# A fused block with 32 heads on one core: values projected as columns and turned by transposes, partly inside the attention, and the front in a new order

## The chip, the cores and the metric

The kernel runs on one core of one Trainium2 chip. Its engines work side by side, each through its own queue of instructions in order: TensorE (PE, with its weight loads shown as PEld), VectorE (DVE), ScalarE (ACT), GpSimd (POOL), and SyncE (SP), whose queue issues all DMAs here. The metric is the device time of one execution in microseconds (us), as the median of several. Lower is better.

## What is computed

The input x has 2048 tokens of 512 columns. A condition c gives six vectors of 512. They shift and scale two layer norms and weigh two residual branches: attention with 32 heads of 16 columns, then a dense layer with GELU and 1792 inner columns.

```python
mod = (_silu(c) @ w_mod).reshape(c.shape[0], 6, 1, -1)
sa, ca, ga, sb, cb, gb = (mod[:, i] for i in range(6))
h = _layernorm(x) * (1 + ca) + sa
qkv = h @ wqkv                      # q, k, v: 32 heads of 16
p = softmax(q k^T * 16 ** -0.5)     # per head, over all 2048 keys
x = x + ga * ((p v) @ wo)
h = _layernorm(x) * (1 + cb) + sb
x = x + gb * (gelu(h @ w1 + b1) @ w2 + b2)
```

All of it is float32. Matmul operands are split into a high and a low part, and three of the four products are added (`terms3`), so a projection of 512 contraction rows is 4 x 3 = 12 matmuls of 128 rows: a group. A group adds up in one PSUM bank of 128 partitions by 512 columns.

## The kernel before

**Front (lines 438 to 547).** For each of four blocks of 512 tokens: `ln1` takes the statistics of the x rows (VectorE, one power on GpSimd) and scales them, `ln1_t` turns them with 16 transposes and evicts them as the high and low parts of h^T (`hT`). Then `proj_qk` forms 128 columns of keys or queries (a chunk, 8 heads) for 512 tokens, with the columns in the partitions, splits them and stores them to DRAM (`qk_d`). `proj_v` forms values for 128 tokens and all 512 columns, with the tokens in the partitions, so four groups serve a block; ScalarE copies each into `vst` (two tiles in turn), which also holds a column of ones per head, and every second copy is stored to `v_d`. All 512 columns of the value weights are loaded at the start into the second x tile (line 185), split by `split_v` and kept in `wv`. The second block of x is loaded into the same tile later (`load_x(1)`, line 485), behind the key and query transfers of the first block.

`quad` (453) runs four groups at once on half the rows: two groups work on opposite halves, and between every 8 half matmuls it may run `mx_pair`: two score matmuls (line 393) whose row maximum VectorE reduces (398). The banks come from rings: `pr` (0, 1, 2, 6, 7) for the front, `mx` (3, 4, 5) for those scores. `XFIRST` orders the first 64 score matmuls of each half. The front ends with 88 of them done (`LEAD`). The maxima of a unit go through DRAM into two extra rows of the query tile, which meet rows of ones (`one_rows`) in the key tiles, so that the exponent is already shifted.

**Attention (lines 551 to 983).** 32 units (four query blocks x eight groups of four heads) of 16 steps, 128 keys each. A step has four score matmuls with an exponential each (589, 594), four score matmuls for the maxima of later units, four products with the values (`pv`, 618), and up to six half matmuls of background work (`RUN`). The background runs through `work()`: `block0` (the remaining keys and queries, 22 groups), then the FFN of blocks 0 to 2. `later(n, f)` runs f after n ticks; a tick is an exponential, so four make a step. `step_start` issues the loads of coming units: first keys at step 1 of a unit, queries at 2, values at 3, second keys at 9. At every third step `prep` loads a piece of wo, w1 or w2, scales and splits it and stores it to DRAM. `open_ffn` (631) frees the memory of the projections for the FFN once `block0` and all `prep` are through. `o_prep` divides an attention output by its sum of exponentials through DRAM (`dn`, `rden`, `rb`); `try_prep` starts one when none is at work (`busy`).

**Tail (from line 986).** What is left of the FFN of block 2 is run together with the last block.

Of the kernel before, what the change touches and what calls it, by code (L numbers as in the profile page):

```python
# [38 lines left out]
XFIRST = [x for r in range(4) for x in [(0, r * 8 + i) for i in range(8)] + [(1, r * 3 + i) for i in range(3)]]  # L39
XFIRST += [(1, i) for i in range(12, 32)]  # L40
RUN = 6
WB = 8
PARTS = ((0, 6), (6, 12), (12, NF))
# [6 lines left out]
def block_kernel(ctx: ExitStack, tc: tile.TileContext, x, wqkv, wo, w1, b1, w2, b2, c, w_mod, out):  # L50
# [78 lines left out]
    wq = [wpool.tile([P, 2, 2, KC, P], FR, name=f"wqk{i}") for i in range(2)]  # L129
    scm, spool = pool("stage", side="right")  # L130
    vcm, vpool = pool("vproj", side="right")
    wv = vpool.tile([P, 2, KC, D], FR, name="wv")
    vst = [vpool.tile([P, NG, 2, VG], F32, name=f"vst{i}") for i in range(2)]

    def stage(name):
        return spool.tile([P, D], F32, tag="s2", name=name, bufs=4)
# [16 lines left out]
    raws = {}  # L153

    def load_w(k):
        raw = pieces("wraw", F32).rearrange("p w (k n) -> p w k n", n=P)
        for w in (1, 0):
            sy.dma_start(raw[:, w], wq_r[:, :, w * D + k * P : w * D + (k + 1) * P])
        raws[k] = raw

    def split_w(k, fast=False):
        raw = raws.pop(k)
        t = wq[k % 2]
        for w in (1, 0):
            if fast:
                ve.tensor_copy(t[:, 0, w], raw[:, w])
                ve.tensor_tensor(t[:, 1, w], raw[:, w], t[:, 0, w].bitcast(F32), op=ALU.subtract)
            else:
                ac.activation(t[:, 0, w], raw[:, w], AF.Copy)
                gp.tensor_tensor(t[:, 1, w], raw[:, w], t[:, 0, w].bitcast(F32), op=ALU.subtract)  # L170

    def split_v():
        for i in range(KC):
            r = xin[1][:, i]
            ac.activation(wv[:, 0, i], r, AF.Copy)
            eng = gp if i % 2 else ve
            eng.tensor_tensor(wv[:, 1, i], r, wv[:, 0, i].bitcast(F32), op=ALU.subtract)
# [5 lines left out]
    load_w(0)  # L183
    for i in range(KC):
        sy.dma_start(xin[1][:, i], wq_r[:, i, 2 * D :])
# [10 lines left out]
    for t in vst:  # L196
        gp.memset(t[:, :, :, 4 * VW :], 0.0)
        for j in range(4):
            gp.memset(t[:, :, :, j * VW + DH], 1.0)
# [5 lines left out]
    def mod_copy(ps):  # L205
        r = stage("mrow")
        ac.activation(r, ps, AF.Copy)
        return r
# [43 lines left out]
    def ln1_t(b, rows, between=lambda: None):  # L252
# [10 lines left out]
        def evac():  # L263
            for fc in range(KC):
                h = stage("h32")
                ac.activation(h, pss[fc], AF.Identity, scale=modc[:, 0, fc, 0:1], bias=modc[:, 0, fc, 1:2])
                e1, e2 = (ve, (ve, gp)[fc % 2]) if b == 0 else (gp, gp)
                e1.tensor_copy(hi[:, fc], h)
                e2.tensor_tensor(lo[:, fc], h, hi[:, fc].bitcast(F32), op=ALU.subtract)
# [7 lines left out]
    def later(n, f):  # L277
        hooks.setdefault(clock["t"] + n, []).append(f)

# [29 lines left out]

    def proj_qk(bk, w, k, b, fast=False):  # L310
        hi, lo = hT[b]
        t = wq[k % 2]

        def evac(ps):
# [4 lines left out]
            else:  # L319
                r = stage("pf")  # L320
                ac.activation(r, ps, AF.Copy)  # L321
                gp.tensor_copy(parts[:, 0], r)  # L322
                gp.tensor_tensor(parts[:, 1], r, parts[:, 0].bitcast(F32), op=ALU.subtract)
            if bk == "bg":
                later(8, lambda: store_qk(w, k, b, parts))
            else:
                store_qk(w, k, b, parts)

        n = range(KC)
        return terms3([t[:, 0, w, i] for i in n], [t[:, 1, w, i] for i in n],  # L330
                      [hi[:, i] for i in n], [lo[:, i] for i in n]), bk, evac

    def proj_v(bk, b, t):
        hi, lo = hT[b]
        sl = slice(t * P, (t + 1) * P)
        kc = b * 4 + t
        v = vst[(kc // 2) % 2]

        def evac(ps):
            ac.activation(v[:, :, t % 2, : 4 * VW].rearrange("p g (j e) -> p g j e", e=VW)[:, :, :, :DH],  # L340
                          ps.rearrange("p (g j d) -> p g j d", j=4, d=DH), AF.Copy)
            if t % 2:
                sy.dma_start(v_d[:, :, kc - 1 : kc + 1, :].rearrange("g p k e -> p g k e"), v)

        n = range(KC)
        return [(hi[:, i, sl], wv[:, j, i]) for i in n for j in range(2)] + [(lo[:, i, sl], wv[:, 0, i]) for i in n], bk, evac
# [85 lines left out]
    def mx_pair():  # L432
        seen = [f() for f in [mx_mm(1), mx_mm(0)]][0]
# [7 lines left out]
    split_w(0, fast=True)  # L441
# [9 lines left out]
    split_v()  # L451
    sy.dma_start(one_d.rearrange("a (x y) -> a x y", y=128), ones[:, None, :].to_broadcast([2, HS // 128, 128]))
    def quad(groups, visits):
# [20 lines left out]

    for b in range(NB):
        run(proj_qk("pr", 1, 0, b, fast=True))
        if b == 0:
            run(proj_qk("pr", 0, 0, 0, fast=True))
        for u in range(2):
            if u == 0 or b < 2:  # L480
                load_k(u, b // 2, (b % 2) * TB, (b % 2 + 1) * TB)
            if b == 0:
                load_q(u)
        if b == 0:
            load_x(1)
        if b + 2 < NB:
            load_x(b + 2)
# [556 lines left out]
```

## Time and profile before

| | |
|---|---|
| median of 3 runs | 1810.22 us (1810.06 to 1820.29) |
| profiled execution | 1813.47 us, span 1811.7 us |
| TensorE busy | 1745.2 us |
| VectorE busy | 1395.3 us |
| ScalarE busy | 1210.0 us |
| first score matmul of the attention proper | at 157.85 us |
| first and last unit's output copied | at 209.72 and 1673.89 us |

The profile lists instructions by engine and source line. A timeline row holds the start, the time, engine, line, operation, the tile written and the tiles read, the shapes, the number of merged instructions, and in brackets how long the engine had been idle and what released it. A row of a group (from the list by lines) holds the total and the mean duration behind the bar. PEclk is the clock that TensorE was granted, as a share of the full one. SP's rows are DMA issues, not transfers. In PE rows the ends are modelled, so starts are compared.

### The profile page before, as it was taken

What the parts mean: (1) busy time and instruction counts of PE and PEld (TensorE: products, weight loads), DVE (VectorE), ACT (ScalarE), POOL (GpSimd) and SP (SyncE); (2) the same over time, 40 slices, a digit from 0 to 9 for tenths busy, and PEclk for the clock granted to TensorE, in tenths of its full rate; (3) what the DMA queues carried; (4) which work ended last, traced back from release to release, by engine and by line L of the source; (5) the groups of instructions that cost most, each with busy time, mean ns of one, the idle gap of its engine ahead of it and who ended that gap; (6) DMA issues with size and microseconds to landing.
All of it is one profiled execution on the core that took longest, in us unless ns stands there. A gap on an engine that the chain in (4) does not pass through costs nothing. (4 is left out here: it accounts for less than half of the span.)

```text
span 1811.7 us, 32267 instructions
## 1 busy us (share of the span) xinstructions
PE 1745.2 (96%) x12020; PEld 902.8 (50%) x12020; DVE 1395.3 (77%) x2341; ACT 1210.0 (67%) x2303; POOL 613.8 (34%) x646
## 2 busy tenths in 40 slices
PE   7698999999999999999999999999999999999899
PEld 5474444444334444444444444444444444444677
DVE  4466888888899888888889988888889988850232
ACT  2424777777677678778776678777777678777031
POOL 2413545443100256306420156405510046503620
PEclk8798999999899999999999999999999999999899
DMA  6648777777653434445447444436546434312544
GB/s 196 202 123 197 206 199 194 205 194 188 174 112 78 84 86 104 84 102 145 114 98 203 100 97 107 91 73 155 120 95 179 117 84 107 91 42 85 201 163 162
DMA packets 122906, 242.62 MB, mean 134 GB/s; under 512 B 30982, under 2 KB 50454, under 8 KB 122750
## 3 DMA queue, kind: packets, MB, share of 16 engines
q1 hardware_dynamic: 122750, 240.57, 51.9%
q8 instruction: 95, 1.56, 0.4%
q14 instruction: 61, 0.50, 0.1%
HBM read 187.61 MB, written 52.90 MB: 133 GB/s over the span
## 5 line engine op out<-in xcount | busy, mean ns | idle before, releaser
L398 DVE TENSOR_REDUCE mxp<-mx 128x1 f32<-128x512 f32 x2048 | 1272.5, 682 | 197.6 <-PE mx L393 168.4
L594 ACT ACTIVATE p<-e 128x512 f32<-128x512 f32 x1964 | 1025.7, 603 | 365.6 <-PE e L589 313.4
L393 PE MATMUL mx<-kh,qst 48*128 48x512 f32 x2048 | 872.0, 443 | 18.6 <-DVE mxp L398 12.3
L589 PE MATMUL e<-qst,kh 50*128 50x512 f32 x1964 | 716.9, 420 | 7.2 <-issue 6.8
L618 PE MATMUL pv<-p,vg 128*32 128x512 f32 x4096 | 549.3, 608 | 0.0
L589 PEld LDWEIGHTS e<-qst,kh 50*128 50x128 f32 x1964 | 357.4, 187 | 178.8 <-ACT p L594 156.1
L393 PEld LDWEIGHTS mx<-kh,qst 48*128 48x128 f32 x2048 | 374.4, 186 | 71.5 <-DVE mxp L398 63.1
L287 PE MATMUL bg<-w,g 64*128 64x512 f32 (+1 forms) x1008 | 271.2, 406 | 2.9 <-DVE x L841 0.4
L287 PE MATMUL bg<-pc,w 64*128 64x512 f32 (+1 forms) x972 | 266.2, 407 | 1.0 <-ACT p L594 0.7
L287 PEld LDWEIGHTS bg<-w,g 64*128 64x128 f32 (+1 forms) x1008 | 177.1, 186 | 144.4 <-ACT p L594 82.2
L287 PEld LDWEIGHTS bg<-pc,w 64*128 64x128 f32 (+1 forms) x972 | 167.6, 184 | 156.9 <-ACT p L594 96.4
L618 PEld LDWEIGHTS pv<-p,vg 128*32 128x32 f32 x4096 | 81.0, 108 | 128.7 <-issue 120.5
L412 POOL CAST m<-mt 128x32 fp32r<-128x32 f32 x32 | 6.7, 210 | 383.3 <-DVE mt L410 383.3
L287 PE MATMUL bg<-hThi,wqk 64*128 64x512 f32 x352 | 107.4, 424 | 0.3 <-ACT p L594 0.3
L815 POOL TENSOR_SCALAR s<-s 128x512 f32<-128x512 f32 x42 | 62.8, 1496 | 128.7 <-ACT s L813 117.9
L287 PEld LDWEIGHTS bg<-hThi,wqk 64*128 64x128 f32 x352 | 59.6, 188 | 80.6 <-ACT p L594 72.2
L287 PE MATMUL bg<-wo,pc 64*128 64x512 f32 x288 | 82.0, 412 | 1.0
L808 POOL TENSOR_TENSOR s<-h 128x512 f32<-128x512 f32 x42 | 43.7, 1040 | 94.1 <-ACT h L807 94.0
L287 PEld LDWEIGHTS bg<-wo,pc 64*128 64x128 f32 x288 | 49.5, 184 | 47.5 <-ACT p L594 27.7
L670 POOL TENSOR_TENSOR ob<-ob,rb 128x512 f32<-128x512 f32 x12 | 15.4, 1284 | 166.8 <-DMA rb<-rden 152.0
L322 POOL CAST parts<-pf 128x512 fp32r<-128x512 f32 x27 | 16.5, 610 | 116.6 <-ACT pf L321 106.3
L816 POOL TENSOR_TENSOR h<-s,h 128x512 f32<-128x512 f32 x42 | 54.0, 1286 | 3.5
(127 smaller groups left out, 1268.5 us busy)
## 6 DMA issues: line engine op xcount, KB each, us to landing
kh<-qk SPq DMA_DIRECT2D x366, 128.0 KB
w<-w1s SPq DMA_DIRECT2D x56, 512.0 KB
w<-w2s SPq DMA_DIRECT2D x50, 512.0 KB
vg<-v SPq DMA_DIRECT2D x32, 664.0 KB
qk<-parts SPq DMA_DIRECT2D x32, 512.0 KB
qst<-qk SPq DMA_DIRECT2D x192, 64.0 KB
ou<-osb SPq DMA_DIRECT2D x32, 256.0 KB
wo<-wos SPq DMA_DIRECT2D x16, 512.0 KB
```

Source lines behind the costliest of these rows:

```text
L287: return te.matmul(ps, term[0][r], term[1][r], start=i == 0, stop=i == n - 1)
L322: gp.tensor_copy(parts[:, 0], r)
L393: te.matmul(ps, qst[u][r0 : r0 + KR, p, qc * P : (qc + 1) * P], kh(u, kr // 2)[r0 : r0 + KR, p, (kr % 2) * TB : (kr % 2 + 1) * TB], start= ...
L398: ins = ve.tensor_reduce(mxp[u][:, hc, kr : kr + 1], ps, axis=AX.X, op=ALU.max, negate=True)
L412: gp.tensor_copy(m2[:, 0], mt)
L589: te.matmul(ps, kh(u, kc // 8)[r0 : r0 + KX, p, (kc % 8) * P : (kc % 8 + 1) * P], qst[u][r0 : r0 + KX, p], start=True, stop=True)
L594: saw(ac.activation(t, ps, AF.Exp, scale=SCALE))
L618: te.matmul(cur["ps"][32 * j : 32 * (j + 1)], vg[u][:, kc, j * VW : j * VW + 32], pt.pop(4 * s + j), start=kc == 0, stop=kc == NKC - 1)
L670: eng.tensor_tensor(ob, ob, rb, op=ALU.mult)
L808: gp.tensor_tensor(s, h, h, op=ALU.mult)
L815: gp.tensor_scalar(s, s, 1.0, None, op0=ALU.add)
L816: gp.tensor_tensor(h, s, h, op=ALU.mult)
```

## The change

Values are now projected like keys and queries: a chunk of 128 columns (8 heads) for 512 tokens, columns in the partitions, the weight chunk stationary. ScalarE copies the bank to an SBUF row tile (`vr`), and `turn_v` turns that by four transposes into one bank, from which two ScalarE copies fill the only tile `vst`, and one DMA stores it. Of the 16 value groups, 8 (chunks 0 and 1) run in the front, 8 (chunks 2 and 3) in the background of the attention; there a turn takes a bank of the `mx` ring and its store goes out 4 ticks later. The queries of blocks 1 and 2 for chunk 0 move from the background to the front. `block0` now follows a plan of 28 groups over ten weight chunks, each loaded two chunks ahead and split 12 ticks later into one of four slots.

The front is no longer a loop over blocks: block 0 with one value group, then `ln1` of blocks 1 and 2, then four quads with keys, values and queries mixed, a last value group and its turns; the last keys, the ones and the values of unit 0 are loaded behind them. The second block of x is loaded at the start. For blocks 1 to 3 the high part of h^T is made by ScalarE from PSUM; front groups' high parts of keys and queries too (both before by GpSimd). `stage` has a tag per use instead of four shared tiles, the tiles of exponentials go from 12 to 10, unit loads are issued at steps 1, 5, 8 and 12, `prep` works 8 ticks after its load, two `o_prep` may be at work, and a callable job of the background no longer uses up its half step.

```diff
-    wq = [wpool.tile([P, 2, 2, KC, P], FR, name=f"wqk{i}") for i in range(2)]
+    wslots = [wpool.tile([P, 2, KC, P], FR, name=f"wqkv{i}") for i in range(4)]
+    vst = wpool.tile([P, 2, 4, VG], F32, name="vst")
...
-    wv = vpool.tile([P, 2, KC, D], FR, name="wv")
-    vst = [vpool.tile([P, NG, 2, VG], F32, name=f"vst{i}") for i in range(2)]
+    wfirst = vpool.tile([P, 2, KC, P], FR, name="wqkv4")
...
-    load_w(0)
-    for i in range(KC):
-        sy.dma_start(xin[1][:, i], wq_r[:, i, 2 * D :])
+    for w in (1, 0):
+        load_w(w, 0)
+    load_x(1)
...
-                e1, e2 = (ve, (ve, gp)[fc % 2]) if b == 0 else (gp, gp)
-                e1.tensor_copy(hi[:, fc], h)
-                e2.tensor_tensor(lo[:, fc], h, hi[:, fc].bitcast(F32), op=ALU.subtract)
+                if b:
+                    ac.activation(hi[:, fc], pss[fc], AF.Identity, scale=modc[:, 0, fc, 0:1], bias=modc[:, 0, fc, 1:2])
+                else:
+                    ve.tensor_copy(hi[:, fc], h)
+                (gp if b or fc % 2 else ve).tensor_tensor(lo[:, fc], h, hi[:, fc].bitcast(F32), op=ALU.subtract)
...
+    def proj_v(bk, k, b):
+        def evac(ps):
+            r = stage("vr")
+            ac.activation(r, ps, AF.Copy)
+            vrows.append((k, b, r, clock["t"]))
+        return proj_terms(2, k, b), bk, evac
+
+    def turn_v(bk):
+        k, b, r, _ = vrows.pop(0)
+        ps = take(bk)
+        for t in range(4):
+            te.transpose(ps[:, t * P : (t + 1) * P], r[:, t * P : (t + 1) * P], ident)
+        v = vst
+        p5 = ps.rearrange("p (t g j d) -> p g t j d", t=4, g=2, d=DH)
+        for g in range(2):
+            ac.activation(v[:, g, :, : 4 * VW].rearrange("p t (j e) -> p t j e", e=VW)[:, :, :, :DH], p5[:, g], AF.Copy)
+        def store():
+            vstored.add((k, b))
+            sy.dma_start(v_d[2 * k : 2 * k + 2, :, 4 * b : 4 * b + 4, :].rearrange("g p k e -> p g k e"), v)
+        if bk == "mx":
+            soon(4, store)
+        else:
+            store()
...
-    for b in range(NB):
...
+    run(proj_qk("pr", 1, 0, 0, fast=True))
+    run(proj_qk("pr", 0, 0, 0, fast=True))
...
+    run(vals(0, 0))
+    rows = ln1(1)
+    ln1_t(1, rows)()
+    load_x(3)
+    rows = ln1(2)
+    turn_v("pr")
+    split_w(1, 1, wslots[1])
+    load_w(2, 1)
+    for _ in range(3):
+        mx_pair()
+    ln1_t(2, rows)()
...
+    quad([keys(1, 0, 1), vals(0, 1), keys(1, 1, 0), keys(1, 1, 1)], [mx_pair] * 3 + [third] + [mx_pair] * 7 + [None])
...
+    ln1_t(3, rows)()
+    turn_v("pr")
...
+    quad([keys(1, 0, 2), vals(0, 2), keys(1, 0, 3), vals(0, 3)], [mx_pair] * 9 + [ahead, mx_pair, None])
...
+    turn_v("pr")
+    turn_v("pr")
+    quad([keys(1, 1, 2), keys(1, 1, 3), keys(0, 1, 0), vals(1, 0)], [mx_pair] * 11 + [None])
...
+    turn_v("pr")
+    quad([vals(1, 1), vals(1, 2), keys(0, 0, 1), keys(0, 0, 2)], [mx_pair] * 8 + [None] * 4)
+    turn_v("pr")
+    turn_v("pr")
+    run(vals(1, 3))
+    turn_v("pr")
...
-    ppcm, ppool = pool("p", bufs=12)
+    ppcm, ppool = pool("p", bufs=10)
...
-        assert not preps and not any(hooks)
+        assert not preps and not owed[0]
...
-        if (unit >= NU - 2 + k // 2 if b == NB - 1 else free_pc[0] >= b) and not busy[0]:
+        if (unit >= NU - 2 + k // 2 if b == NB - 1 else free_pc[0] >= b) and busy[0] < 2:
...
+        plan = [(1, 2, range(NB)), (0, 2, [0]), (2, 2, range(NB)), (1, 3, range(NB)), (0, 3, [0]), (2, 3, range(NB))]
+        plan += [(0, 0, [3])] + [(0, k, range(1, NB)) for k in range(1, KC)]
...
+                while vrows and clock["t"] >= vrows[0][3] + 4:
+                    yield lambda: turn_v("mx")
...
-        if kc == 2 and u + 2 < NU:
+        if kc == 5 and u + 2 < NU:
             load_q(u + 2)
-        if kc == 3 and u + 1 < NU:
+        if kc == 8 and u + 1 < NU:
             load_v(u + 1)
-        if kc == 9 and u + 2 < NU:
+        if kc == 12 and u + 2 < NU:
             load_k(u + 2, 1)
```

`soon` is `later` with a count of what is still owed, on which `open_ffn` now waits instead of on every hook; `keys(w, k, b)` and `vals(k, b)` are `proj_qk` and `proj_v` in the front's ring; `third` is a `mx_pair` with `ln1(3)` behind it, `ahead` one with a key load before it.

245 lines of the change are left out of this document (115 added, 130 removed).

## The prediction

> **What bounds the kernel now.** I read the page's busy times first, then a table of stages (windows), then the timeline around each hole that the table shows, and last the waits of the DMA queue.
>
> ```profile
> span 1811.7 us, 32267 instructions
> PE 1745.2 (96%) x12020; PEld 902.8 (50%) x12020; DVE 1395.3 (77%) x2341; ACT 1210.0 (67%) x2303; POOL 613.8 (34%) x646
> ```
>
> The stages:
>
> ```profile
> 38.00:49.00 11.00, 0.33 (x1) 0.18 (x1) 5.02 (x14) 1.20 (x2) 1.01 (x1) 0.59 0.90 283
> 49.00:71.00 22.00, 16.46 (x70) 10.45 (x69) 3.00 (x10) 13.00 (x19) 13.48 (x15) 0.66 0.61 184
> 71.00:92.00 21.00, 15.98 (x120) 12.74 (x119) 17.18 (x35) 4.15 (x7) 5.74 (x6) 0.92 0.63 203
> 150.30:157.90 7.60, 0.75 (x6) 0.35 (x5) 0.69 (x1) 0.70 (x2) 1.78 (x3) 0.66 0.74 274
> 209.70:256.40 46.70, 46.70 (x354) 22.79 (x356) 40.08 (x67) 35.66 (x70) 21.20 (x23) 1.00 0.77 199
> 441.70:491.00 49.30, 46.38 (x258) 18.86 (x260) 40.47 (x69) 33.84 (x66) 5.48 (x7) 0.90 0.71 181
> 491.00:535.00 44.00, 42.15 (x258) 16.67 (x260) 40.27 (x68) 33.52 (x66) 4.93 (x7) 1.00 0.48 103
> ```
>
> The first score and the first product with values (pv):
>
> ```profile
> 157.85 0.76 PE L589 MATMUL e<-qst,kh 50*128 50x512 f32 x1 [6.85 <-issue]
> 164.29 0.20 PEld L618 LDWEIGHTS pv<-p,vg 128*32 128x32 f32 x8 [0.65 <-issue]
> ```
>
> Columns of a window: length, then busy time of PE, PEld, DVE, ACT and POOL, granted clock, DMA share, GB/s. TensorE bounds most of it. A unit of the attention (16 steps) with background work in every step takes 46.70 us, all of it PE (2.92 a step); the unit without any takes 44.00 (2.75 a step). The front, up to the first score at 157.85, has three holes: 38 to 49, the half clock after it, and 150 to 158.
>
> **The front, followed through.** Its rows:
>
> ```profile
> 25.77 2.02 PE L287 MATMUL pr<-wv,hThi 128*128 128x512 f32 x8
> 42.16 0.69 DVE L227 BATCH_NORM_STATS2 bst<-xin 128x6 f32<-128x512 f32 x1 [14.86 <-DMA xin<-in_A_x_dram]
> 47.80 2.93 ACT L249 ACTIVATE xin<-xin,nb,rs 128x512 f32<-128x512 f32 x4 [10.03 <-DVE nb L247]
> 48.67 0.18 PEld L260 LDWEIGHTS pr<-ident,xin 128*128 128x128 f32 x1 [11.98 <-ACT xin L249]
> L266 ACT ACTIVATE h<-pr,modc 128x512 f32<-128x512 f32 x16 | 11.9, 776 | 2.6 <-DVE modc L216 1.4 <-PE pr L260 0.6
> L269 POOL TENSOR_TENSOR hTlo<-h,hThi 128x512 fp32r<-128x512 f32 x14 | 18.4, 1315 | 10.6 <-DVE hThi L268 9.6
> L232 POOL TENSOR_TENSOR rs<-rs,mhalf 128x4 f32<-128x4 f32 x4 | 4.1, 1014 | 30.5 <-DVE rs L231 30.5
> 84.42 0.28 PEld L393 LDWEIGHTS mx<-kh,qst 48*128 48x128 f32 x1 [5.46 <-DVE mxp L398]
> 91.96 2.11 PE L287 MATMUL pr<-hThi,wqk 128*128 128x512 f32 x8
> 94.82 1.91 PE L260 MATMUL pr<-ident,xin 128*128 128x128 f32 x16
> 113.95 1.92 PE L203 MATMUL pr<-wm,s_m 128*32 128x512 f32 x16
> 118.59 1.20 PE L287 MATMUL pr<-wv,hThi 64*128 64x512 f32 x8
> 132.60 0.39 PE L287 MATMUL pr<-hThi,wqk 64*128 64x512 f32 x1
> ```
>
> Prices from them: a group of 12 full matmuls 2.86 us (91.96 to 94.82); a quad of four groups with 22 score matmuls 14.0 (118.59 to 132.60), 1.17 a visit; 16 transposes 1.9; a modulation with its broadcast 4.6 (113.95 to 118.59).
>
> Keys and queries of block 0 stay, to 25.7. Four value groups become one: PE is done at 28.6. The second block of x now takes the place of the value weights in the first loads, so VectorE starts its statistics behind the query's subtraction at about 27.3, not at 42.16; 5.2 us later (47.80 less 42.16, less a DMA wait of 0.45) the rows are scaled, and the transposes start at 33.4. The hole of 11.5 us shrinks to 4.9. Then other engines set the pace. Each part of h passes ScalarE twice (0.78 each, the high part no longer on POOL) and POOL once (1.3); block 2's power waits on POOL behind four such subtractions: 42.4 (36.2 and eight passes) + 1.3, then the power 1.0 and the factors 0.5, give 45.3. Its transposes end near 50.2; the first quad starts at 51.3 when a ring bank is free. It keeps the stall that the row at 84.42 shows, since statistics still sit among the score reductions (some 4.3 of 5.5; x is there earlier), with an estimated 3.5 for the clock at its start and after the stall (its window of 21.0 us holds 14.0 of work and 5.5 of stall, so 1.5 went there, and now it starts cold): 51.3 + 14.0 + 7.8 = 73. The second quad waits for bank evictions: two key groups (four passes of 0.6), one split (0.65) and four of block 3's passes on ScalarE: start 79, end 93.5. Modulation and two turns 4.7, third quad 14: 112. Modulation with broadcast and a turn 5.1: 117.5. The last quad has 8 visits with scores and 4 without: 13.2, to 130.7.
>
> Behind it comes a chain that is new. The values are turned through one tile (before: two), so a turn's copies wait until the previous store has read it.
>
> ```profile
> 96.37 0.36 SPq L308 DMA_DIRECT2D qk<-parts  x1
> 99.35 2.66 SPq L364 DMA_DIRECT2D kh<-qk  x6
> 136.29 5.38 SPq L364 DMA_DIRECT2D kh<-qk  x6
> 141.71 6.62 SPq L370 DMA_DIRECT2D kh<-one  x10
> 154.95 0.57 SPq L423 DMA_DIRECT2D qst<-m  x2
> L340 ACT ACTIVATE vst<-pr 128x512 f32<-128x512 f32 x16 | 9.0, 600 | 36.7 <-PE pr L287 22.7 <-issue 14.0
> ```
>
> A store lands some 2.5 us after its issue (96.73 to 99.35). Three turns are left: copies 0.8 (two halves of the 0.60 row's size, estimated at 0.4 each), issue 0.4, landing 2.5, so 3.7 each. First store at 135.2 (behind the query evictions), third at 142.6. Behind it the same queue issues the last keys (5.4 us) and the ones (6.6), then the value load. The first pair of ones lands near 151.6 (issue to use 2.3 us, from 155.52 to 157.85): first score 6 us earlier than 157.85. The value load goes out at 155 and is larger; at 4 us it lands at 159.3, and the first pv matmul, wanted at 158.0, runs there instead of at 164.29. **Front: -5.0 us.** The maxima of unit 0 are done by 126 now, so their transfer, on which 157.85 waited, is hidden.
>
> **Background in the attention.** Eight value groups come in, two query groups (blocks 1 and 2 of chunk 0) go to the front: 6 x 24 = 144 half matmuls, and one group less is left for the tail (24): 168, at 6 a step 28 steps, from 2.75 to 2.92 us. **+4.6 us.** They fill the steps between the end of the projections and the FFN of block 0, which waits for unit 7 either way; it starts no later.
>
> **Turns in the attention.** Eight, each 4 transposes: 1.91/4 = 0.48 us on a PE that has no room. Their ScalarE copies (0.8) fit a gap:
>
> ```profile
> 175.74 0.60 ACT L594 ACTIVATE p<-e 128x512 f32<-128x512 f32 x1 [0.85 <-PE e L589]
> ```
>
> ScalarE waits 0.85 us at each step's start, just when a turn's copies come. Lower end 0.4, upper end 1.3 (copies added in full); I take 0.54: **+4.3 us** (range 3 to 10). Ten weight chunks are now split there too (before four); POOL is at 21 of 46.7 us, so its part costs nothing while it keeps that room.
>
> **Opening of the FFN pools.** Before, it came right behind the last prepared weights:
>
> ```profile
> 452.76 1.76 SPq L743 DMA_DIRECT2D x<-in_A_x_dram  x4
> 458.89 0.35 DVE L658 RECIPROCAL dn<-dn 128x32 f32<-128x32 f32 x1 [2.41 <-DMA dn<-ou]
> 1673.78 8.47 PE L287 MATMUL bg<-pc,w 128*128 128x512 f32 x36
> 1690.34 1.62 PE L287 MATMUL bg<-wt,g 128*128 128x512 f32 x3 [5.33 <-POOL s L815]
> 1702.50 0.69 DVE L670 TENSOR_TENSOR ob<-ob,rb 128x512 f32<-128x512 f32 x1 [7.19 <-DMA rb<-rden]
> ```
>
> VectorE stood 2.4 us behind dn, TensorE's clock fell (0.90 in that unit) and the unit took 49.3 instead of 44.0. With the projections 19 steps longer, the weights are long stored; what is in flight is one key or query store (2.5 us), so dn lands in time. **-4.0 us** (0 to -5.3). Two of these outputs may now be in work at once; k=3, which the FFN waits for, starts at unit 7's end as before.
>
> **Tail.** One group of 12 fewer: 8.47/3 = 2.8 us of PE, and POOL's chain, which stopped PE for 5.3 at 1690, is a tile ahead; but the divided output of the last unit, at 1702.5 behind DMAs, comes when it came. **-3.0 us** (0 to -7). The later issue of the key, query and value loads is costed at nothing: a unit of 46.70 us with PE at 46.70 waits for no load now, and they keep 4 to 8 steps of cover (11 to 23 us); without it, each late load stops PE in full.
>
> Sum: -5.0 + 4.6 + 4.3 - 4.0 - 3.0 = -3.1 us on a profiled execution of 1813.47 (span 1811.7); on the median of 1810.22 that is 1807.
>
> **A rule weighed.** Do the transposes ahead of the first quad wake the clock?
>
> ```profile
> 64.20:67.20 3.00, 2.95 (x13) 2.64 (x13) 0.69 (x1) 2.70 (x5) 1.51 (x2) 0.50 0.30 113
> 67.20:70.90 3.70, 2.89 (x25) 1.35 (x24) 0.00 (x0) 2.52 (x5) 3.54 (x5) 0.98 0.32 103
> 157.90:164.30 6.40, 6.14 (x27) 4.01 (x27) 4.15 (x6) 3.77 (x7) 3.39 (x4) 0.50 0.70 216
> ```
>
> Here 3 us of nothing but transposes were followed by a clock of 0.98, while 6.4 us of scores and groups at the attention's start stayed at 0.50. If transposes woke nothing, the first quad would lose half of up to 6.4 us at its start, 3.2 us: 1810. The Trainium skill, "TensorE: Matmul & The Clock Gate", section "Part 4: PE-mode transpose", says that transposes do not count as busy in the way matmuls do; the trace (0.98 behind thirteen transposes) disagrees.
>
> **Rivals.** (A) Slower: ScalarE waits in the attention for DMAs. A turn's copies wait for the previous store, a split for its weights, and all later exponentials queue behind them. 8 turns and 10 splits make 18 waits; past the gap of 0.85 us each is paid in full and slows the clock. At 1.5 us each: 1807 + 27 = 1834; it decides (over 1%) from 1.2 us each. For it: SP blocked for 6 us around 446 to 452. Against: a store has 11.6 us to the next turn (four steps), a weight chunk 8.7 to its split (12 ticks, 4 a step). 0.10. (B) The front's waits for banks, ScalarE and stores take the whole gain: 1807 + 5 = 1812. 0.20. (C) The end chain hides and the front is bound by PE alone: PE's work ends at 134, first score near 140, -18 instead of -5: 1794, and with the upper ends of opening and tail 1788. 0.13. (D) the cold quad, 1810: 0.05.
>
> **Numbers.** My sum has 0.52; time 1807. Low is C with its middle, 1794; high is 1822, which takes B with turns at 1.3 us (+6) and no gain at the opening (+4). About 1% is what a measurement of this kernel can tell from no change: faster than 1792 only in most of C (0.10), slower than 1828 only in A (0.10), between them 0.80. The sum, B and D lie well inside.
>
> **What would show it.** The first score near 152 and first pv near 159; a PE hole of about 5 us at 28 to 33; three value stores some 3.7 us apart near 135 to 143; units of 46.7 us up to the seventh, plus 0.5 for each turn; no DVE wait at dn when the FFN opens; 520 matmuls behind the last pv against 532. Units far above 47 us with ACT waiting on DMA would prove A; a first score before 143 would prove C.

## The result, and the profile after

The changed kernel takes 1837.74 us (median of 4 runs, 1835.94 to 1839.31), the kernel before 1812.99 in the same comparison (4 runs, 1810.06 to 1820.29): ratio 1.013, 95% interval 1.0095 to 1.0165. It is slower by about 1.3%. The forecast was 1807 us, with 1794 to 1822 as its range. The profiled execution of the changed kernel took 1835.94 us.

The head of its page:

```profile
span 1834.2 us, 32758 instructions
PE 1748.8 (95%) x12168; PEld 911.3 (50%) x12168; DVE 1388.4 (76%) x2336; ACT 1235.7 (67%) x2361; POOL 612.3 (33%) x631
```

The span grew by 22.5 us, PE's busy time by 3.6 only. The other 18.9 us are PE idle: 66.5 us before (1811.7 less 1745.2), 85.4 after. So the question is who makes TensorE wait, and where.

The ends of stages are the starts of the units' output copies (osb from pv): unit 0's at 209.72 before and 210.59 after, unit 4's at 395.93 and 409.62, unit 6's at 490.96 and 502.83, unit 8's at 581.18 and 603.29, the last unit's at 1673.89 and 1697.61.

| stage | before | after | change | forecast |
|---|---|---|---|---|
| to unit 0's output | 209.7 | 210.6 | +0.9 | -5.0 |
| units 1 to 4 | 186.2 | 199.0 | +12.8 | +4.6 |
| units 5 and 6 | 95.0 | 93.2 | -1.8 | -1.6 |
| units 7 and 8 | 90.2 | 100.5 | +10.3 | +1.8 |
| units 9 to 31 | 1092.7 | 1094.3 | +1.6 | 0 |
| behind the last | 137.8 | 136.6 | -1.2 | -3.0 |

The last column is the forecast's sum laid out by stage, which is done here and not in the prediction (by rounding it adds up to -3.2, the sum was -3.1): background +0.3, +1.0, +2.7 and +0.5 us in unit 2, unit 5, unit 6 and units 7 and 8 (steps filled up, 0.17 us each), the turns in units 1 to 4, and the opening's cost of 5.3 us gone from unit 6 and back in unit 7 with 1.3. Three stages hold the miss: the turns, the opening of the FFN, the front.

Windows by unit in the changed kernel (units 1 to 4, 7 and 8; columns as in the windows above: length, PE, PEld, DVE, ACT, POOL, granted clock, DMA share, GB/s):

```profile
210.59:259.11 48.52, 47.73 (x358) 23.15 (x360) 40.11 (x66) 37.18 (x74) 22.29 (x24) 1.00 0.71 191
259.11:310.11 51.00, 49.41 (x366) 24.17 (x368) 40.21 (x66) 37.90 (x76) 17.09 (x19) 1.00 0.71 192
310.11:356.76 46.65, 46.65 (x354) 22.71 (x356) 40.04 (x66) 36.62 (x72) 22.29 (x24) 1.00 0.75 206
356.76:409.62 52.86, 50.48 (x370) 24.61 (x372) 40.31 (x66) 38.56 (x78) 16.32 (x18) 1.00 0.57 151
...
502.83:555.49 52.66, 47.28 (x276) 19.61 (x276) 40.73 (x69) 34.45 (x67) 9.06 (x11) 0.89 0.67 181
555.49:603.29 47.80, 46.86 (x300) 20.81 (x302) 41.59 (x70) 33.75 (x65) 6.37 (x8) 0.94 0.51 105
```

The third unit here has no turn and takes 46.65 us, PE all busy, as forecast. The others have 1, 3 and 4 turns (4 matmuls each over 354) and take 1.9, 4.4 and 6.2 us more: 1.55 us a turn. Unit 7 has little background (276 matmuls) and still takes 52.66.

ScalarE's waits in the changed kernel (engine, line, waited for: total us, times, longest):

```profile
ACT vst L367 <- DMA v<-vst: 22.9, 3, 15.8
...
ACT vr L353 <- PE mx L363: 10.1, 6, 1.7
```

The second row is the turns: six times, 1.7 us each, the copy of a value group into its row tile waits for a turn. The timeline at one of them:

```profile
378.88 0.66 PE L363 MATMUL mx<-ident,vr 128*128 128x128 f32 x4
...
379.57 0.60 ACT L353 ACTIVATE vr<-bg 128x512 f32<-128x512 f32 x1 [1.69 <-PE mx L363]
...
380.06 1.08 ACT L645 ACTIVATE p<-e 128x512 f32<-128x512 f32 x2
380.22 0.49 PE L296 MATMUL bg<-hThi,wqkv 64*128 64x512 f32 x1 [0.69 <-ACT vr L353]
```

The order of these four is the mechanism. Group n+1 is done, and ScalarE's next instruction copies it into `vr`, of which the attention has one. That buffer is free when group n has been turned, and TensorE's order puts that turn behind the end of group n+1 and the pv of the step. So ScalarE stands 1.69 us, two exponentials stand behind the copy, and TensorE then waits as well (0.69 us at 380.22). The fourth turn of a chunk has no value group behind it and no such wait.

### The profile page after: what moved, and what is told of

It is laid out like the page before. It is cut to its first block, busy times and chain, and to the rows that moved or that the text cites. A ratio compares the mean times of both kernels' runs of the same rounds, so it can differ in the third digit from the quotient of the medians.

```text
span 1834.2 us, 32758 instructions
## 1 busy us (share of the span) xinstructions
PE 1748.8 (95%) x12168; PEld 911.3 (50%) x12168; DVE 1388.4 (76%) x2336; ACT 1235.7 (67%) x2361; POOL 612.3 (33%) x631
## 5 line engine op out<-in xcount | busy, mean ns | idle before, releaser
L645 ACT ACTIVATE p<-e 128x512 f32<-128x512 f32 x1991 | 1043.3, 603 | 364.1 <-PE e L640 310.9
L640 PE MATMUL e<-qst,kh 50*128 50x512 f32 x1991 | 728.1, 417 | 11.4 <-DMA kh<-one 11.1
L640 PEld LDWEIGHTS e<-qst,kh 50*128 50x128 f32 x1991 | 365.1, 187 | 160.1 <-ACT p L645 132.0
L423 PEld LDWEIGHTS mx<-kh,qst 48*128 48x128 f32 x2048 | 378.7, 187 | 67.2 <-DVE mxp L428 55.4
L296 PE MATMUL bg<-hThi,wqkv 64*128 64x512 f32 x448 | 135.5, 419 | 4.1 <-ACT vr L353 4.1
L296 PEld LDWEIGHTS bg<-hThi,wqkv 64*128 64x128 f32 x448 | 74.2, 184 | 101.3 <-ACT p L645 87.5
L296 PE MATMUL bg<-hTlo,wqkv 64*128 64x512 f32 x224 | 61.1, 392 | 0.0
L296 PE MATMUL pr<-hThi,wqkv 64*128 64x512 f32 (+1 forms) x288 | 53.0, 427 | 3.9 <-ACT hThi L263 2.0
L869 POOL TENSOR_TENSOR g<-h,g 128x512 fp32r<-128x512 f32 x42 | 54.0, 1286 | 3.4
```

The lines of the kernel that those rows point to most:

```text
L296: return te.matmul(ps, term[0][r], term[1][r], start=i == 0, stop=i == n - 1)
L423: te.matmul(ps, qst[u][r0 : r0 + KR, p, qc * P : (qc + 1) * P], kh(u, kr // 2)[r0 : r0 + KR, p, (kr % 2) * TB : (kr % 2 + 1) * TB], start= ...
L640: te.matmul(ps, kh(u, kc // 8)[r0 : r0 + KX, p, (kc % 8) * P : (kc % 8 + 1) * P], qst[u][r0 : r0 + KX, p], start=True, stop=True)
L645: saw(ac.activation(t, ps, AF.Exp, scale=SCALE))
L869: gp.tensor_tensor(g[:, 1], h, g[:, 0].bitcast(F32), op=ALU.subtract)
```

## The turns: two experiments

**Left out.** The transposes and copies are not done, the store still is (the values of chunks 2 and 3 are then not the right ones):

```diff
-        ps = take(bk)
-        for t in range(4):
-            te.transpose(...)
+        if bk != "mx":
+            ps = take(bk)
+            ...
-        for g in range(2):
+        for g in range(2 if bk != "mx" else 0):
```

> The changed kernel with its eight turns inside the attention left out: the four transposes and the two copies of each are not done, the store is still issued (so the values of chunks 2 and 3 of each row are not the right ones). Theory 1 (a turn costs what it makes ScalarE wait for: the next group's copy stands behind the turn because there is one buffer for the untransposed rows) and rival 2 (a turn costs its own instructions) both expect units 1 to 4 (the ends of their output copies) at 186 to 188 us in place of 199.0, and some 11 to 13 us less in all, about 1825. Rival 3 (units 1 to 4 are longer because loads, splits or value groups came in, not for the turns): units 1 to 4 stay at 195 to 199, and the total at 1834 to 1838.

Measured: 1826.37 us, ratio to the kernel before 1.0076 (1.0051 to 1.0101); units 1 to 4 took 186.6 us, what they took before the change, with the ten splits, the value groups and the later loads all in. The total is 11.4 us less. Rival 3 falls: all 12.4 us are the turns.

**Earlier.** The turn goes to the start of a half step inside the next group:

```diff
+        if vrows and clock["t"] >= vrows[0][3] + 4:
+            turn_v("mx")
         if act["g"] is None:
```

> The changed kernel with each turn issued at the start of the half step that is at least four ticks behind its group, in the middle of the next group, not behind that group's end. All instructions stay. Theory 1: the next group's copy finds its buffer free, the wait of 1.69 us in six of eight turns goes, a turn is left with 0.5 of PE: units 1 to 4 at 189 to 191 us in place of 199.0, total 8 to 10 us less, about 1828. Rival 2 (the turn's own instructions on PE and ScalarE are the cost, wherever it stands): units 1 to 4 at 197 to 200, total 1836 to 1839. In between, 192 to 196, if the two copies on ScalarE push the exponentials by themselves.

Measured: 1832.51 us, 1.011 (1.0088 to 1.0131); units 1 to 4 took 191.5, half a us above what theory 1 gave. Who waits for the turn's transposes (the view of their source line), in the changed kernel and then here:

```profile
who waited for it (us, times):
  ACT vr L353: 10.1, 6
  ACT vst L367: 0.4, 2
```

```profile
who waited for it (us, times):
  ACT vst L367: 4.2, 6
```

The wait of the next group's copy is gone; only the turn's own copies wait. Of the 12.4 us, 7.5 were the wait (199.0 to 191.5) and 4.9 what a turn costs without it (191.5 to 186.6), 0.61 each. The forecast had 0.54 for it. The total fell by 5.2 us only, not by the 8 to 10 of theory 1: behind unit 4 this execution took 3 us more, 2.7 of them in unit 30 (on such units see the last section).

## The opening of the FFN: one prep, other loads, another queue

SP's issues in unit 7 of the changed kernel (timeline of the DMA queue), and VectorE at the same time:

```profile
531.84 0.61 SPq L717 DMA_DIRECT2D rb<-rden  x1
...
533.08 0.61 SPq L717 DMA_DIRECT2D rb<-rden  x1
...
535.04 7.33 SPq L394 DMA_DIRECT2D kh<-qk  x6
542.41 0.63 SPq L699 DMA_DIRECT2D dn<-ou  x1
```

```profile
545.83 0.35 DVE L709 RECIPROCAL dn<-dn 128x32 f32<-128x32 f32 x1 [5.05 <-DMA dn<-ou]
```

The six key issues take 7.33 us, where six of them in the front took 2.80 (the row at 150.82 further below). The third output's dn stands behind them, and VectorE, which executes in order, stops 5.05 us at the reciprocal: the score reductions queue behind it, and TensorE stops (no matmul from 543 to 545) and runs at half clock from 545 to 560.

The queue's own waits tell where the 7.33 us went. Here are SP's longest one from 535 to 542.4 (as in the list of waits above), what POOL waited for at its end, and the window in between:

```profile
SPq L394 <- DMA rb<-rden: 4.5, 1, 4.5
```

```profile
542.12 1.27 POOL L721 TENSOR_TENSOR ob<-ob,rb 128x512 f32<-128x512 f32 x1 [2.94 <-DMA rb<-rden]
```

```profile
537.00:541.00 4.00, 3.79 (x24) 1.67 (x22) 3.27 (x6) 3.01 (x6) 2.04 (x3) 1.00 1.09 165
```

Five key loads are out by 537.5. The sixth stands until the second preparation's rb, issued at 533.08, has landed, 9 us after its issue, while the DMA engines are busy throughout (share 1.09). So the transfers themselves are late, and the queue hands that on. Why a key load has to wait for an rb load at all stays open: the kernel's text gives no reason. With one preparation at a time the six issues took 4.28, with the loads at their old steps 7.35, 3.8 of it behind ob loads. The kernel before has such a row too (8.30 us at 486.50), but there the dn went out ahead of it, at 483.36, and VectorE did not wait.

**One preparation at a time**, as before the change (`busy[0] < 2` becomes `not busy[0]`):

> The changed kernel with one output preparation in work at a time again (before the change: one; after: two). Theory 1: unit 7 is 8 us too long because three preparations' transfers crowd one queue, and the third one's dn stands behind the key load: with one at a time unit 7 takes 45 to 47.5 us in place of 52.7, total 5 to 8 us less, 1830 to 1833. Rival: the key load at step 12 meets the output's transfers whatever their number, and the later start of the second and third preparation moves the stall into the same or the next unit: units 7 and 8 together stay at 98 to 101 us (measured 100.5), no change in the total.

Measured: 1837.68 us, 1.0136 (1.0112 to 1.0159). Both theories were half right. The windows of units 7 and 8 (here from the ends of the output copies) and of what lies behind the last unit:

```profile
507.31:551.80 44.49, 43.09 (x276) 17.78 (x273) 40.42 (x69) 34.17 (x67) 5.51 (x7) 1.00 0.67 185
551.80:596.20 44.40, 42.81 (x270) 17.58 (x269) 40.49 (x69) 33.50 (x65) 9.97 (x11) 1.00 0.61 139
1688.07:1833.30 145.23, 128.23 (x538) 101.55 (x538) 40.18 (x59) 28.84 (x43) 46.89 (x42) 0.94 0.50 169
```

The stall is gone: 88.9 us for the two units in place of 100.5, full clock. But the four outputs are now divided one behind the other: the fourth dn goes out 17.9 us behind unit 7's output, not 6.8. The FFN starts later (270 matmuls in unit 8, not 300), and the work that this pushes out is done behind the last unit: 538 matmuls and 145.2 us there, in place of 520 and 136.6. With a slower front in this execution (214.4), nothing is left. Before the change, one at a time as well, the pools opened in unit 6 (the x load at 452.76), and the fourth dn went out 5.3 us behind unit 7's output; now they open in unit 7 (515.79).

**The loads at their old steps** (2, 3 and 9 in place of 5, 8 and 12):

> The changed kernel with the loads in the attention at the steps that they had: queries at step 2 (not 5), values at 3 (not 8), the second half of the keys at 9 (not 12). Theory 1: the second half of the keys no longer falls on the second and third output's transfers in unit 7 (its six issues took 7.3 us there, and dn stood behind them): unit 7 at 45 to 48 us in place of 52.7, units 1 to 4 unchanged (198 to 200), total 5 to 7 us less. Rival (the opening of the FFN's pools costs what it did before, 4 to 5 us, wherever the loads are): unit 7 at 49 to 53, total within 2 us.

Measured: 1840.01 us (1832.52 to 1847.99, the widest spread of all), 1.0149 (1.0111 to 1.0188): no gain, and too uncertain to tell a few us. Unit 7 took 46.3, as theory 1 said, but unit 8 took 50.5 (47.8 without the edit); there VectorE waited 3.07 us on the fourth dn.

**Another queue.** The transfers of the preparations issued by POOL (`gp.dma_start` for dn, ob, rden and rb):

> The changed kernel with the four transfers of each output preparation (dn, ob, rden, rb) issued from POOL's queue, not SP's; two in work at a time as in the changed kernel, same steps. Theory 1 (dn stood behind the key load on SP's queue, not on the DMA engines): no wait of VectorE on dn above 1 us, unit 7 at 45 to 47 us in place of 52.7, unit 8 at 45 to 47 in place of 47.8, FFN starts where it did, total 6 to 9 us less (about 1830). Rival 1 (the DMA engines are what is full at 530 to 550, not the queue): dn is as late, unit 7 at 50 to 54. Rival 2 (a stall that goes in unit 7 comes back where the FFN's first weights load, as with one preparation): unit 7 shorter, units 8 and 9 or the stretch behind the last unit longer by as much, total within 2 us.

Measured: 1860.65 us, 1.026 (1.0237 to 1.0283), a miss for every total that was forecast. POOL's timeline and VectorE's:

```profile
539.03 0.63 POOL L717 DMA_DIRECT2D rb<-rden  x1 [6.44 <-DMA rden<-dn]
...
545.97 1.26 POOL L721 TENSOR_TENSOR ob<-ob,rb 128x512 f32<-128x512 f32 x1 [5.53 <-DMA rb<-rden]
...
549.18 0.62 POOL L699 DMA_DIRECT2D dn<-ou  x1
```

```profile
552.92 0.35 DVE L709 RECIPROCAL dn<-dn 128x32 f32<-128x32 f32 x1 [9.43 <-DMA dn<-ou]
```

POOL executes in order too. The next dn stands behind the wait for rden, the wait for rb and the division, and VectorE waits 9.43 us. Three openings of an FFN block paid for it (units 7, 15 and 24 took 56.7, 54.8 and 54.5). The six key loads on SP took 9.30 us here too, without the preparations in their queue: 6.2 of them were waits for wo loads, and the DMA share from 529 to 538 was 0.99. That bears out the first half of rival 1 (the DMA engines are full). A change of queue does not make the transfers land earlier, and on POOL its own waits came on top.

**The reciprocal later.** It is written 16 ticks behind its transfers, not 10, for the first three outputs:

```diff
-        later(10, inv)
+        later(10 if k == KC - 1 else 16, inv)
```

> The changed kernel with VectorE's reciprocal of the first three outputs of each block placed 16 ticks behind the issue of their transfers, not 10 (the last output keeps 10). With POOL's queue the transfers came later still, so the queue is not the cure; what is left of theory 1: VectorE executes in order, and the reciprocal is written at a fixed place, 7.3 us behind an issue that took 8 us more. With 16 ticks (11.7 us) the wait of 5 us on dn goes, and the third preparation starts 4 us later, clear of the key load: unit 7 at 45 to 47 us in place of 52.7, units 8 and 9 as they are, FFN some 4 us later at most, total 4 to 7 us less (about 1832). Rival (the stall is only moved, since the transfers are what is slow): unit 7 shorter, but units 8, 9 and the stretch behind the last unit longer by as much: within 2 us of 1838.

Measured: 1833.91 us, 1.01 (1.0075 to 1.0124). Unit 7 took 44.7, but, as the rival said, unit 8 took 52.6 (47.8 without the edit), where the reciprocal of the fourth output waited 2.24 us, and unit 9 53.4. The two units give 3 us, and the gain of 4 us on the median is within what unit 9's clock alone can move (last section).

## The front: its order, and a second tile

The DMA queue in two stretches of the changed kernel's front, ScalarE behind the first, and the two first matmuls:

```profile
106.41 0.94 SPq L151 DMA_DIRECT2D wm<-in_w_mod_dram  x2
107.45 9.35 SPq L371 DMA_DIRECT2D v<-vst  x2
...
```

```profile
143.02 7.75 SPq L371 DMA_DIRECT2D v<-vst  x3
150.82 2.80 SPq L394 DMA_DIRECT2D kh<-qk  x6
153.67 6.59 SPq L400 DMA_DIRECT2D kh<-one  x10
160.44 0.35 SPq L595 DMA_DIRECT2D vg<-v  x1
```

```profile
115.75 0.66 ACT L367 ACTIVATE vst<-pr 128x256 f32<-128x256 f32 x2 [15.77 <-DMA v<-vst]
```

```profile
159.76 0.76 PE L640 MATMUL e<-qst,kh 50*128 50x512 f32 x1 [11.05 <-DMA kh<-one]
...
164.66 0.23 PEld L669 LDWEIGHTS pv<-p,vg 128*32 128x32 f32 x8 [0.64 <-issue]
```

Two things stand out. A turn's copies waited from 99.98 until 115.75 for the previous turn's store. That store was issued only at 107.45, since SP had key loads and two modulation weights of 1 MB each ahead of it, and it took another 8.3 us with these weights in flight (in the window from 109 to 112 the DMA share was 1.03). The evictions of the third quad and the modulation stood behind them on ScalarE. And the end chain (three stores, keys, ones, value load) runs one behind the other to 160.44, so the first pv came at 164.66, where it was before.

**The order at the end.** The ones ahead of the third quad, the value load ahead of the last keys:

```diff
-    load_k(1, 1)
-    for k in khalf:
-        one_rows(k)
...
+    for k in khalf:
+        one_rows(k)
     quad([keys(1, 1, 2), keys(1, 1, 3), keys(0, 1, 0), vals(1, 0)], ...)
...
     load_v(0)
+    load_k(1, 1)
+    for k in khalf[3:]:
+        one_rows(k)
```

> The changed kernel with two steps of the front's end moved on the queue: the rows of ones of all five key buffers are sent ahead of the third quad (buffers 4 and 5 once they exist, behind the values), and the first unit's values are loaded ahead of the last keys, right behind the last value store. Theory 1 (the chain of stores, keys, ones and value load on one queue sets the first pv): the value load goes out near 151 in place of 160.4, the first pv comes near 155 in place of 164.7, unit 0's output near 201 in place of 210.6, total 8 to 10 us less (about 1829). Rival 1 (the quads, the banks and the turns set the front's end, the queue's rest is hidden): the first pv stays within 2 us of 164.7, total 1835 to 1839. Rival 2: the last keys now come late for the maxima of unit 1 (needed some 7 us after the start), and half of the gain is lost: unit 0's output near 206, total 1833.

Measured: 1834.62 us, 1.0113 (1.0094 to 1.0133). The first pv came at 155.36, as theory 1 said, but unit 0's output at 204.0, 6.6 us earlier, not 9.6 (rival 2 had 206, for late keys; TensorE waited 0.65 us for them). The attention starts at a colder clock. The first 15 us from the first score, in the changed kernel and then here:

```profile
159.76:174.76 15.00, 14.72 (x74) 7.69 (x78) 11.56 (x19) 10.46 (x21) 4.46 (x4) 0.71 0.78 191
```

```profile
149.32:164.32 15.00, 13.08 (x47) 6.84 (x47) 7.99 (x14) 7.88 (x16) 1.28 (x1) 0.50 0.88 190
```

The total gave 3 of these 6.6; unit 9 took 56.2 in the profiled execution, in place of 50.4, at a clock of 0.85.

**Two tiles for the turned values** (the selector of the modulation lies in the b2 tile, to make room):

```diff
-    vst = wpool.tile([P, 2, 4, VG], F32, name="vst")
+    vst = [wpool.tile([P, 2, 4, VG], F32, name=f"vst{i}") for i in range(2)]
...
-        v = vst
+        v = vst[nturn[0] % 2]
+        nturn[0] += 1
```

> The changed kernel with two tiles for the turned values in place of one (the selector of the modulation lies in the b2 tile for that). Theory 1 (ScalarE stands 15.8 us at 99 to 115 before a turn's copies and 5.2 and 2.0 at 146 to 150, for the previous store to read the one tile, and the evictions and the modulation stand behind it): modulation and fourth quad start some 5 us earlier, the last three stores follow within 4 us, first pv near 156 to 159 in place of 164.7, total 6 to 8 us less (about 1831). Rival (PE has only 3.3 us idle between 115 and 140, so the wait is nearly covered, only the tail of the stores shortens): first pv 161 to 163, total 2 to 3 us less.

Measured: 1833.54 us, 1.01 (1.0076 to 1.0125). The three last stores were issued from 136.74 on (4.65 us, in place of 143.02 and 7.75), the first pv came at 157.86, 6.8 us earlier, as theory 1 said. Unit 0's output was only 3.2 us earlier (the clock stood at 0.50 for 20 us from the first score), and the total 4.2 less, between theory 1 and its rival.

**The kernel before with the new order at the end:**

> The kernel before, with the front's end in the order of the fifth experiment: the rows of ones of the first three key buffers sent ahead of the last value quad, the first unit's values loaded ahead of the last keys. Theory 1 (in the kernel before the maxima of unit 0 and their transfer, issued near 155, set the first score at 157.85, so the order of the rest is hidden; it became the path only with the change): first score within 2 us of 157.85, first pv 160 to 164, total 1 to 4 us less than the kernel before. Rival (the same chain bound both kernels, the change only lengthened it): first pv near 155, total 7 to 9 us less.

Measured: 1807.5 us, ratio 0.9973 (0.9956 to 0.999). Its first score:

```profile
155.85 0.76 PE L591 MATMUL e<-qst,kh 50*128 50x512 f32 x1 [3.91 <-DMA qst<-m]
```

Theory 1 holds for the path: there the maxima of unit 0 (qst from m) set the start, and the order of the rest is hidden behind them; the first score came 2 us earlier and the first pv at 162.29. The total is 4.9 us less by the ratio, more than theory 1 gave and less than its rival. That chain became the path only when the change took the maxima off it. The small gain over the kernel before is real by its interval: 2.1 us of it in the front, some 1 each in units 6 and 9 in the profiled executions.

## All mended

**Turn, order and second tile together:**

> The changed kernel with three edits together: the turn in the middle of the next group, the front's order at the end (ones early, values ahead of the last keys), two tiles for the turned values. If the causes stand side by side, their gains add: 5.2 (measured for the turn) + 8 to 10 + 2 to 8, total 1814 to 1823, that is within 0.6% of the kernel before, first pv near 148 to 154. If the two edits of the front take away the same wait, the sum is the larger one: 1822 to 1825.

Measured: 1816.82 us (10 runs), 1.0011 (0.9998 to 1.0023), as the first branch said. Units 1 to 4 took 191.2, unit 0's output came at 197.1: 13.5 us earlier than in the changed kernel, more than 6.6 and 3.2 together. The first pv, at 148.11, came 16.6 us earlier, and there the two gains add (9.3 and 6.8): the edits shorten one chain at its two ends. Between first pv and output the two single edits lose 2.7 and 3.6 us, and both together lose 3.1: the loss, with the clock at 0.50 for the first 15 us in all three, is paid once. It was not traced further. The total fell by 21 us, what the stages give (13.5 and 7.8 in units 1 to 4), and more than the three single gains on the medians (5.2, 3.1, 4.2); in the profiled executions of the single edits, unit 9 (56.2 and 53.8 with the two of the front) and unit 30 (some 2.6 longer in all three) had taken a part.

**And the reciprocal late, three of four, then all four, then the loads back:** `later(10 if k == KC - 1 else 16, inv)`, then `later(16, inv)`, then the queries at step 2, then all loads at their old steps.

> The three mended places together (turn in the middle of the next group, order of the front's end, two tiles for turned values) and the reciprocal of the first three outputs at 16 ticks. If the opening's stall is on the path: unit 7 at 45 to 47 in place of 53.1, total 1809 to 1813, at or a little under the kernel before (ratio 0.997 to 1.001). If it comes back behind the last unit: 1815 to 1818.

> The eleventh kernel with the reciprocal of all four outputs of a block at 16 ticks (the last one too, at which VectorE waited 3.8 us in unit 8 of the eleventh). If that wait was on the path: unit 8 at 46 to 47 us in place of 51.5, FFN 4 us later at most (6 to 12 matmuls fewer in unit 8, 1.5 to 3 us more behind the last unit), total 1808 to 1811. If what is saved comes back as later FFN work behind the last unit: 1812 to 1814.

> The twelfth kernel with the query load of the attention at step 2 (as before the change), not 5. If the late query load is what stopped TensorE in unit 8 (1.75 us at 553.35, then half clock to about 565, some 5 us in all): unit 8 at 46 to 47.5 us in place of 51.6, total 1806 to 1809, ratio 0.996 to 0.999. If the stall only goes on to the next late transfer: units 7 to 10 together within 2 us of the twelfth's 194.4, total 1811 to 1814.

> The twelfth kernel with all three loads at their steps before the change (queries 2, values 3, second half of the keys 9). If the later loads were the cause and nothing else hangs on them: as the thirteenth or 1 us better, 1805 to 1809. If the keys at step 9 fall on the rb loads of the first two outputs (in the fourth experiment their six issues took 7.4 us at 523.5 too): unit 7 one to three us longer than the thirteenth's, total 1808 to 1812.

Measured: 1812.65 us, 0.9991 (0.9978 to 1.0003); 1812.75, 0.9997 (0.9979 to 1.0016); 1811.64, 0.999 (0.9972 to 1.0008); 1811.23, 0.9992 (0.9978 to 1.0007). All stand level with the kernel before and with each other. Unit 7 took 44.7, 44.8, 45.6 and 44.7; unit 8 took 51.5, 51.5, 51.8 and 51.3. So the eleventh came as its first branch said, unit 7 and total both. The twelfth, thirteenth and fourteenth missed what their theories gave for unit 8 or the total; the thirteenth came as its rival said (units 7 to 10 at 195.4). The fourteenth's total lies in its rival's range, but its unit 7 was shorter than the thirteenth's, not longer. What ended the wait in unit 8 of the twelfth kernel, and then of the last:

```profile
553.35 0.69 PE L425 MATMUL mx<-kh,qst 48*128 48x512 f32 x2 [1.75 <-DMA qst<-qk]
```

```profile
545.62 0.35 DVE L713 RECIPROCAL dn<-dn 128x32 f32<-128x32 f32 x1 [3.12 <-DMA dn<-ou]
```

With all reciprocals late it is the queries; with the queries earlier it is a dn again (3.02 us in the thirteenth too). Each cure tried here handed the wait to another transfer. Only one preparation at a time took it out of both units, and that pushed the FFN's work behind the last unit. One preparation at a time together with the three mended places was not run, and whether an order exists that pays neither stays open.

## Why the prediction was wrong, step by step

- **Bound by PE, units of 46.7 us; background +4.6; 520 matmuls behind the last pv.** Right: units 3, 5 and 6 took 46.65, 46.60 and 46.61, and 520 it was. (28 steps at 0.17 are 4.7, not 4.6; nothing hangs on it.)
- **Turns +4.3 (0.54 each): failed by a missing wait.** "Their ScalarE copies (0.8) fit a gap" asked only what a turn issues, and for that it was nearly right (0.61 measured). It did not ask who waits for the turn. With one row tile, the next value group's copy does, and the exponentials behind that copy: 7.5 us of the 12.4.
- **Opening -4.0, "dn lands in time": failed.** Units 7 and 8 took 10.3 us more than before, the forecast allowed 1.8. "What is in flight is one key or query store" left out that two preparations bring their own transfers (five each: dn, two ob, rden, rb), that the second half of the keys falls among them, and that SP and VectorE keep their order: the sixth key load stood 4.5 us for an rb, the dn behind it came late, and VectorE stood 5.05 us. The forecast named the edit to two preparations and costed only what it meant at unit 7's end; with one at a time the stall is gone (88.9 us for the two units). The later loads, put at nothing, cost nothing up to unit 6; in unit 8 of the twelfth kernel the queries stopped TensorE for 1.75 us.
- **Front -5.0: failed by the time to one store's landing, and by taking the first pv for the output.** The forecast went step by step to 93.5 for the end of the second quad, and the trace agreed within 2 us or so (transposes at 35.45 against 33.4, first quad at 52.41 against 51.3, third at 99.6 against 98.2). Then "a store lands some 2.5 us after its issue": the one ahead of the modulation was issued 7.5 us after its copies and took 8.3 more, with two weight loads in front of it. The copies waited 22.9 us in all, and the fourth quad came at about 125 in place of 117.5. From there the chain ran a little faster than forecast (17.4 us from the first of the last three stores to the value load, not 19.8), but from 143.02, not from 135.2, and the first pv came at 164.66 in place of 159. That this chain sets the first pv was right (first pv at 155.36 with its order changed). That an earlier first pv brings the output forward by as much was not: with two tiles the first pv came at 157.86, and unit 0's output still at 207.4, 2.3 us earlier than before the change, not 5.0 or more.
- **Tail -3.0**: mis-sized; -1.2, with 3.8 us less PE work (122.17 against 125.93) and 2.5 us more idle.
- **Rivals.** A gave 1834, and the time came near it for another reason: ScalarE did wait in the attention, but for TensorE, not for DMAs, and A's count was off: eight turns at 1.55 us, and no cost for the ten splits (units 1 to 4 at 186.6 without turns), so 12 us, not 27; the rest came from front and opening. B was right on the front alone. C, the hidden end chain, had its first score near 140 only with the front mended (140.88). D fell: the first quad was not cold,

```profile
48.00:52.00 4.00, 4.00 (x17) 3.48 (x17) 1.82 (x4) 4.00 (x8) 1.56 (x2) 0.50 0.23 85
52.00:56.00 4.00, 4.00 (x33) 3.17 (x32) 2.12 (x4) 3.65 (x6) 3.86 (x4) 0.94 0.24 66
```

  sixteen transposes at 0.50 were followed by the first quad at 0.94. Three score matmuls (from 46.89) ran just ahead of these transposes, so the rows do not show that the transposes alone woke the clock; and in the eighth kernel twenty transposes and three scores (33.89 to 41.05) left it at 0.50. By the Trainium skill, "TensorE: Matmul & The Clock Gate", "Part 4: PE-mode transpose", transposes do not count as busy in the way matmuls do; these rows settle nothing beyond that of the kernel before (0.98 behind thirteen transposes).

## What to carry to other kernels

When an operation is split into "fill a buffer" and "empty it" on two engines that keep their order, ask first where the emptying stands in the other engine's order, and what queues behind the next fill: here one buffer cost more than the operation itself (7.5 us and 4.9), and moving the emptying a half group earlier took that away without memory. A landing time read off a quiet queue (2.5 us) was a lower end where large loads were issued ahead on the same queue (8.3), and the wait for the issue came on top (7.5). When issues on a queue take long, read the queue's own waits: they named the transfer. When the wait that set a stage's start is taken away, look at once for the next chain that ends there: an order that was free before (ones and values last) became the path.

## What the hardware showed beside that

Short holes cost a clock in one execution and not in another. Unit 9 runs the FFN's first transposes, with 318 matmuls and 2.5 us of PE idle in the changed kernel and 2.1 in the fifth experiment. The two stretches around the same hole, in the changed kernel and then in that experiment:

```profile
628.30:633.30 5.00, 4.26 (x29) 2.02 (x27) 4.37 (x9) 3.64 (x7) 0.01 (x1) 1.00 0.01 3
633.30:638.30 5.00, 4.20 (x26) 1.37 (x25) 4.71 (x9) 2.66 (x5) 2.60 (x4) 1.00 0.57 95
638.30:643.30 5.00, 4.66 (x32) 2.07 (x32) 4.74 (x9) 3.78 (x8) 3.01 (x2) 1.00 1.02 159
```

```profile
620.00:625.00 5.00, 3.84 (x25) 1.54 (x21) 4.62 (x10) 4.02 (x8) 0.46 (x2) 1.00 0.01 3
625.00:630.00 5.00, 4.72 (x17) 1.88 (x17) 3.40 (x8) 1.56 (x4) 2.72 (x2) 0.54 0.68 111
630.00:635.00 5.00, 5.00 (x21) 1.84 (x24) 3.29 (x6) 2.78 (x6) 2.44 (x2) 0.50 0.99 177
635.00:640.00 5.00, 5.00 (x24) 1.64 (x16) 3.75 (x7) 2.07 (x4) 0.00 (x0) 0.50 0.49 196
```

The one keeps the full clock, the other falls to half for some 15 us, and the unit takes 56.2 us in place of 50.4. The changed kernel and the second, fifth and sixth experiments differ only ahead of unit 5. From unit 5 on their profiled executions differ by up to 5.8 us in unit 9, by 1.1 to 2.7 in units 7, 8, 18 and 30, and by 0.3 at most in any other. So a gain of 3 us here is read from the stage and not from the total. The Trainium skill, "TensorE: Matmul & The Clock Gate", "Part 1: The HAM clock gate", says that the clock is decided in a window that runs freely and does not start with the kernel. The rows are in keeping with that, and no run here tested it.
